# Four stacked attention blocks on one core: bulk loads on a second DMA queue, weights also in idle key and value tiles, softmax denominators normalised per head group

## The chip, the cores and the metric

The kernel runs on one NeuronCore of one Trainium2 chip. The metric is device time in microseconds (us) of one execution, lower is better. Engine names as in the profile: PE is TensorE (matmuls), PEld its weight loads, ACT ScalarE, DVE VectorE, POOL GpSimd, SP SyncE, which here does nothing but issue DMAs.

## The reference

The input `x` has 2048 rows (tokens) of 1024. Two kinds of block alternate, A, B, A, B, each with a layer norm in front and a residual sum behind, and both A blocks share one set of weights, as do both B blocks.

```python
def _A_ref(x, wqkv, w_phi, wo):            # H = 32 heads of Dh = 32
    q, k, v = split(x @ wqkv)
    pq = einsum("bhsd,hdf->bhsf", q, w_phi); pk = einsum("bhsd,hdf->bhsf", k, w_phi)
    phi_q = concat([softmax(pq), softmax(-pq)]); phi_k = concat([softmax(pk), softmax(-pk)])
    kv = einsum("bhsf,bhsd->bhfd", phi_k, v);  z = einsum("bhsf->bhf", phi_k)
    o = einsum("bhqf,bhfd->bhqd", phi_q, kv) / (einsum("bhqf,bhf->bhq", phi_q, z)[..., None] + 1e-6)
    return o @ wo
def _B_ref(x, wqkv, wo):
    q, k, v = split(x @ wqkv)
    p = softmax(einsum("bhqd,bhkd->bhqk", q, k) * Dh ** -0.5)
    return einsum("bhqk,bhkd->bhqd", p, v) @ wo
x = x + _A_ref(_layernorm(x), ...);  x = x + _B_ref(_layernorm(x), ...)     # and both once more
```

A is linear attention: it needs one sum over all tokens (`kv`, `z`) before the first query can be answered. B is ordinary softmax attention over all 2048 keys, 32 heads.

## The kernel before, in words

**How the order comes about.** The kernel is one Python function that plays a clock while it emits instructions (class `Clock`, lines 110 to 190). Each piece of work is a generator that yields operations with an assumed duration and, for DMAs, an assumed latency (`DMA_LAT`, 2.2 us, line 33; 5 or 6 us for the big ones). An operation is written to its engine's stream when the played clock gets there. Every engine, SP's and POOL's streams included, then runs its stream strictly in that order; a wait on the chip that is longer than was assumed holds up everything behind it.

**The layers.** Layers 0 and 2 are A blocks, 1 and 3 are B blocks. Tokens go in four chunks of 512 (`c`), which are 16 tiles of 128 (`t`). For an A block `build_AK` (line 622) computes keys and values of a chunk and adds to `kv`, `build_PQ` (747) the queries, `build_DN` (770) numerator and denominator, `build_AO` (867) the output projection. For a B block `build_BP` (885) makes keys (tiles `K2a`, `K2b`), queries (written to DRAM, `qd`) and values (`Vc`), and `build_BO` (1047) does the output projection. At the very start `build_fold` (564) multiplies `w_phi` into the key and query weights of A; the raw weights lie in the value tiles `Vc` meanwhile, and the products go to DRAM (`wf`).

**Attention of a B block.** It goes in 18 visits (`VISITS`, line 210), each a group of 4 or 2 query tiles against some key chunks for half of the heads: 8 units of two heads each. A unit's step is two exponentials (ACT, line 1187) of 128 x 1024, with the score matmuls ahead (PE, line 1207, into the `ring` banks) and value and row-sum matmuls behind (PE, line 1243, into the one bank `acc`). `finish_unit` (978) then empties `acc` through DVE: line 990 copies, or line 986 (a helper, shown as L351) adds a partial result that `part_load1` fetched from DRAM (`pd`). A unit that isn't its query group's last stores its partial result to `pd`. Visits 9 to 18 are "last": there the row sums of each unit go by DMA to DRAM (`dn`), back to 128 partitions (`rc`, two DMAs, line 1012), through one DVE reciprocal (line 1015), to DRAM again (`rn`, two DMAs, line 1017), back as a broadcast into a buffer `R` (two DMAs, lines 1021 and 1023), and POOL multiplies the result into `oTB` (line 1033). The DMAs wait one for the other on SP. Visits 13 and 14 are the shortest "last" ones: query group 3 against key chunk 3 alone, 2 steps a unit.

**Background.** All other matmuls (projections) are a list of tasks; `pick` (1281) takes the first that has its inputs and its weights. Of the weights, which come as blocks of 1 MB (`slab`), four are held; `slab_plan` (503) loads the one that is needed next into the place of the one that is needed last.

**Queues.** Every DMA is issued by SP (`dma`, line 332), the 1 MB loads among them; the transposes of layer-normed tiles too (336). POOL issues none. POOL does the power for the layer norm's 1/sqrt (412), additions in `build_DN` (846) and the normalisation. Work buffers of 2 KB a partition (`blk`, 23 of them) are shared; tokens limit how many of them one kind of use may hold (`t_acc` 3, `t_part` 4, `t_R` 3, line 307).

## Time and profile before

| | us |
|---|---|
| median of the runs shown (2) | 2794.26 (2788.96 to 2799.56) |
| the profiled execution, time of the run | 2795.94 |
| the profiled execution, span | 2794.2 |
| busy in the span: PE, ACT, DVE, POOL | 2321.4, 2095.9, 977.9, 277.6 |
| DMA: bytes, mean rate | 329.84 MB, 118 GB/s |

The span is one execution, from the first instruction to the last. Engine times are sums over stages that are limited by different things, so the prediction reads them stage by stage: the A block ahead of the first attention (0 to 289), attention of layer 1 (289 to 1506), the A block between (1506 to 1668), attention of layer 3 (1668 to 2781) and the end. Within attention the stages are cut at visits. In a row of such a table a number in brackets behind an engine's busy time counts its instructions; the last three numbers are the granted TensorE clock as a share of full speed, the DMA engines' mean busy share, and GB/s.

### The profile page before, as it was taken

The page shows a single profiled execution, that of the slowest core. Times are in us where ns is not written, and L with a number is a line of the kernel's source. Part 1 is how long each engine was busy: PE and PEld are TensorE (multiplying, and loading weights), DVE is VectorE, ACT ScalarE, POOL GpSimd, SP SyncE. Part 2 cuts the span into 40 slices and gives each one's busy share as a digit, 9 for nine tenths or more (in the row PEclk, how much of TensorE's full clock was granted, in tenths as well). Part 3 has the DMA queues.
Part 4 walks back from the last instruction along what each step waited for, and adds up shares of the span by engine and source line. Part 5 has one row for each costly group of instructions (what it writes and reads, how often), then busy time and mean ns, then how long its engine had stood idle before and what let it go on. Part 6 is the DMA issues. An engine that isn't in the chain of part 4 may idle for free. (4 is left out here: it accounts for less than half of the span.)

```text
span 2794.2 us, 67944 instructions
## 1 busy us (share of the span) xinstructions
PE 2321.4 (83%) x28313; PEld 922.3 (33%) x28313; DVE 977.9 (35%) x1885; ACT 2095.9 (75%) x2413; POOL 277.6 (10%) x327
## 2 busy tenths in 40 slices
PE   6987888988998887677888679889899888877888
PEld 4443332333332222233334333333333322123333
DVE  6866431523332133433333654234233221111011
ACT  4341479789998988477996216778799999957998
POOL 1102000101001111110000010000010011111010
PEclk9999998999998798888999889989999978666787
DMA  7334743553443333533125566347434333332111
GB/s 228 90 106 142 208 161 116 160 173 92 130 127 103 104 97 106 142 96 82 40 48 150 167 177 206 128 138 188 135 100 149 98 100 93 90 92 66 36 29 29
DMA packets 376533, 329.84 MB, mean 118 GB/s; under 512 B 174312, under 2 KB 313440, under 8 KB 370976
## 3 DMA queue, kind: packets, MB, share of 16 engines
q1 hardware_dynamic: 376224, 325.50, 40.7%
q8 instruction: 221, 3.62, 0.6%
q14 instruction: 88, 0.72, 0.1%
HBM read 227.86 MB, written 72.34 MB: 107 GB/s over the span
## 5 line engine op out<-in xcount | busy, mean ns | idle before, releaser
L1187 ACT ACTIVATE E<-ring 128x1024 bf16<-128x1024 f32 x2048 | 1920.7, 1101 | 327.6 <-PE ring L1207 235.2
L1243 PE MATMUL acc<-E,V 128*32 128x512 bf16 (+1 forms) x5120 | 720.3, 385 | 82.8 <-DVE blk L351 68.4
L1243 PE MATMUL acc<-E,ones 128*32 128x512 bf16 (+1 forms) x5120 | 720.1, 385 | 0.0
L1207 PE MATMUL ring<-Q,K2b 32*128 32x512 bf16 (+1 forms) x2560 | 446.3, 376 | 149.8 <-ACT E L1187 143.4
L1207 PE MATMUL ring<-Q,K2a 32*128 32x512 bf16 (+1 forms) x2560 | 464.3, 377 | 39.9 <-DMA Q<-qd 27.2
L1243 PEld LDWEIGHTS <-V 128*32 128x32 bf16 x5120 | 212.8, 102 | 395.9 <-issue 364.8
L351 POOL TENSOR_TENSOR oTB<-blk,blk 64x512 bf16<-64x512 f32 (+1 forms) x156 | 167.0, 1071 | 1131.0 <-DMA blk<-rn 1042.8
L1207 PEld LDWEIGHTS <-K2a 32*128 32x128 bf16 x2560 | 123.7, 93 | 464.0 <-issue 423.7
L1207 PEld LDWEIGHTS <-K2b 32*128 32x128 bf16 x2560 | 148.4, 93 | 268.0 <-issue 259.0
L1015 DVE RECIPROCAL rc<-rc 128x8 f32<-128x8 f32 (+1 forms) x156 | 30.1, 193 | 573.3 <-DMA rc<-dn 573.1
L365 PE MATMUL bg<-xnT,slab 128*32 128x512 bf16 x2604 | 190.8, 414 | 28.0 <-ACT blk L758 9.7
L1243 PEld LDWEIGHTS <-ones 128*32 128x32 bf16 x5120 | 203.5, 102 | 0.1
L990 DVE COPY blk<-acc 128x512 f32<-128x512 f32 (+1 forms) x160 | 93.2, 582 | 268.3 <-PE acc L1243 266.4
L365 PEld LDWEIGHTS <-slab 128*32 128x32 bf16 x4232 | 121.1, 101 | 172.8 <-issue 88.7
L365 PE MATMUL bg<-slab,xnT 128*32 128x512 bf16 x1940 | 146.0, 424 | 30.9 <-DVE kvacc L351 10.6
L351 DVE TENSOR_TENSOR blk<-blk,acc 128x512 f32<-128x512 f32 x128 | 87.5, 683 | 228.8 <-PE acc L1243 158.0
L351 POOL TENSOR_TENSOR blk<-blk 128x256 bf16<-128x256 f32 x96 | 70.0, 733 | 754.3 <-DVE blk L351 404.5
L368 PE MATMUL ring<-slab,xnT 128*128 128x512 bf16 x464 | 114.0, 387 | 9.9 <-DVE kvacc L351 2.6
L351 DVE TENSOR_TENSOR blk<-blk,bg 128x512 bf16<-128x512 bf16 x110 | 75.3, 684 | 129.0 <-PE bg L365 115.7
L365 PE MATMUL bg<-kvacc,slab 128*32 128x512 bf16 x1580 | 109.0, 391 | 12.6 <-DVE K2b L346 9.3
L365 PE MATMUL bg<-slab,oTB 128*32 128x512 bf16 x1500 | 108.7, 413 | 10.0 <-DVE blk L351 8.9
L368 PEld LDWEIGHTS <-xnT 128*128 128x128 bf16 x795 | 77.9, 99 | 114.1 <-issue 17.7
(111 smaller groups left out, 1927.7 us busy)
## 6 DMA issues: line engine op xcount, KB each, us to landing
slab<-in_B_wqkv_dram SPq DMA_DIRECT2D x48, 1024.0 KB
pd<-blk SPq DMA_DIRECT2D x128, 256.0 KB
blk<-pd SPq DMA_DIRECT2D x128, 256.0 KB
slab<-in_A_wo_dram SPq DMA_DIRECT2D x16, 1024.0 KB
Q<-qd SPq DMA_DIRECT2D x256, 64.0 KB
slab<-wf_pq SPq DMA_DIRECT2D x14, 1024.0 KB
Q<-qd SPq DMA_DIRECT2D x112, 128.0 KB
x<-blk SPq DMA_DIRECT2D x48, 256.0 KB
```

Source lines behind the costliest of these rows:

```text
L351: return ("op", e, cost, lambda x: eng(x).tensor_tensor(out=o, in0=a, in1=b, op=op))
L365: nc.tensor.matmul(o[js], lhsT=l[:, js], rhs=r, start=st, stop=sp, tile_position=(0, 32 * j), skip_group_check=True)
L368: nc.tensor.matmul(o, lhsT=l, rhs=r, start=st, stop=sp, skip_group_check=True)
L990: yield ("op", "V", c_ps(n), lambda e: nc.vector.tensor_copy(out=a, in_=acc_t[:, 0:n]))
L1015: yield ("op", "V", 0.2, lambda e: nc.vector.reciprocal(out=rc[:, 0:m], in_=rc[:, 0:m]))
L1187: yield ("op", "S", c_act(2 * n), lambda x: nc.scalar.activation(out=E[:, :, 0:n], in_=ring_t[buf][:, :, 0:n], func=ACT.Exp, scale=INV_SQR ...
L1207: nc.tensor.matmul(ring_t[bufs[e]][:, j, i * n:(i + 1) * n], lhsT=K2[e][c][r, u.g, m, :], rhs=u.Q[r, e, 0:n], start=True, stop=True, tile_ ...
L1243: nc.tensor.matmul(u.acc[r0 + 32 * j:r0 + 32 * j + 32, 0:n], lhsT=lh, rhs=E[:, j, i * n:(i + 1) * n], start=first, stop=final, tile_positi ...
```

## The change

It has three parts, and new numbers for the played clock. (1) `bulk` issues weight loads, the spills of layer-normed activations and their reloads on POOL's DMA queue; all smaller DMAs stay on SP. (2) The value and key tiles are split by halves of the heads, and while they aren't needed for keys and values, each group of them serves as a further place for weights (`Slot`, `slot_open`, `slot_retire`); a task that writes keys or values first retires the place. `slab_plan` may look at 12 blocks ahead in place of 6. (3) `norm` treats the two units of a head group together: their four rows of sums go through one chain, and the broadcast reciprocals land in the unused halves of the two result buffers, so `R` goes. `oTB` tiles become `blk` buffers, of which there are 28; `t_acc` is 5, `t_part` 6. The folded weights' order at the start, the place of `build_PQ(2, 0)` and the assumed durations change as well.

```diff
-DMA_LAT = 2.2
+DMA_LAT = 2.4
+RATE = {"D": 200e3, "P": 150e3}
...
-    return (124 + n) / 960.0
+    return (150 + n) / 960.0
...
-    return 0.2 + 0.0034 * n
+    return 0.18 + 0.0022 * n
...
-    K2 = [[sb(f"K2{x}{c}", [P, G, 2, P]) for c in range(NC)] for x in "ab"]
-    Vc = [sb(f"V{c}", [P, 4, D]) for c in range(NC)]
+    K2 = [[[sb(f"K2{x}{c}{h}", [P, 4, 2, P]) for h in range(2)] for c in range(NC)] for x in "ab"]
+    Vc = [[sb(f"V{c}{h}", [P, 4, C]) for h in range(2)] for c in range(NC)]
...
+    slots = [Slot([sb(f"slab{i}", [P, PO, C])[:]], 8, True) for i in range(4)]
+    vs_no, ks_no = {}, {}
+    for h in range(2):
+        for i in range(2):
+            vs_no[h, i] = len(slots)
+            slots.append(Slot([Vc[2 * i + j][h][:] for j in range(2)], 4, False))
+            ks_no[h, i] = len(slots)
+            slots.append(Slot([K2[x][2 * i + j][h][:].rearrange("p g m n -> p (g m n)").rearrange(
+                "p (a n) -> p a n", n=C) for j in range(2) for x in range(2)], 2, False))
...
-    t_q, t_acc, t_part, t_R, t_tmp = tok(2), tok(3), tok(4), tok(3), tok(3)
+    t_q, t_acc, t_part, t_R, t_tmp, t_ot = tok(2), tok(5), tok(6), tok(2), tok(3), tok(8)
...
-    def dma(o, i, lat=DMA_LAT):
-        return ("op", "D", 0.07, lambda e: nc.sync.dma_start(out=o, in_=i), lat)
+    qbusy = {"D": 0.0, "P": 0.0}
+
+    def queue(q, kb):
+        def lat():
+            qbusy[q] = max(qbusy[q], clk.now) + kb * 1024 / RATE[q]
+            return qbusy[q] - clk.now + DMA_LAT
+        return lat
+
+    def dma(o, i, kb=4):
+        return ("op", "D", 0.07, lambda e: nc.sync.dma_start(out=o, in_=i), queue("D", kb))
+
+    def bulk(o, i, kb):
+        return ("op", "P", 1.0, lambda e: nc.gpsimd.dma_start(out=o, in_=i), queue("P", kb))
...
-        yield dma(slab_t[i][:], src, 6.0)
+        n = len(sl.parts)
+        for j, part in enumerate(sl.parts):
+            ld = bulk(part, src[:, j * sl.per:(j + 1) * sl.per, :], 1024 // n)
+            yield ld if j == n - 1 else ld[:4] + (0.0,)
...
+    def slot_retire(i):
+        sl = slots[i]
+        if not sl.avail:
+            return True
+        if sl.users or sl.loading:
+            return False
+        for x in [x for x in slab_of if slab_of[x] == i]:
+            del slab_of[x]
+            slab_ready.pop(x, None)
+        sl.avail = False
+        return True
...
-            yield dma(dnd[i][:, 0:n], a[d0:d0 + 64:32, :])
-            for j in range(2):
-                yield ("op", "D", 0.07, lambda e, j=j: nc.sync.dma_start(
-                    out=rc[64 * j:64 * j + 64, 0:m], in_=dnd[i][j, 0:n].rearrange("(p e) -> p e", e=m)),
-                    DMA_LAT * j)
-            yield ("op", "V", 0.2, lambda e: nc.vector.reciprocal(out=rc[:, 0:m], in_=rc[:, 0:m]))
-            for j in range(2):
-                yield ("op", "D", 0.07, lambda e, j=j: nc.sync.dma_start(
-                    out=rnd[i][j, 0:n].rearrange("(p e) -> p e", e=m), in_=rc[64 * j:64 * j + 64, 0:m]),
-                    DMA_LAT * j)
-            rc_s.give(rc)
-            yield ("op", "D", 0.07, lambda e: nc.sync.dma_start(
-                out=r[n0:n0 + 32, :], in_=rnd[i][0:1, 0:n].to_broadcast([32, n])), 0.0)
-            yield dma(r[n0 + 32:n0 + 64, :], rnd[i][1:2, 0:n].to_broadcast([32, n]))
...
+    def norm(x0, x1):
+        u, a0, tk0, b0 = x0
+        _, a1, tk1, b1 = x1
...
+        yield ("op", "D", 0.07, lambda e: nc.sync.dma_start(out=dn[0:2, :], in_=a0[64:128:32, :]), 0.0)
+        yield dma(dn[2:4, :], a1[0:64:32, :], 20)
+        yield dma(rc[:, 0:m], dn[:].rearrange("a (p e) -> (a p) e", e=m), 20)
+        yield ("op", "V", 0.2, lambda e: nc.vector.reciprocal(out=rc[:, 0:m], in_=rc[:, 0:m]))
+        yield dma(rn[:].rearrange("a (p e) -> (a p) e", e=m), rc[:, 0:m], 20)
+        rc_s.give(rc)
+        for j in range(4):
+            dst = (a1[32 * j:32 * (j + 1), :] if j < 2 else a0[32 * j:32 * (j + 1), :])
+            yield ("op", "D", 0.07, lambda e, j=j, dst=dst: nc.sync.dma_start(
+                out=dst, in_=rn[j:j + 1, :].to_broadcast([32, n])), queue("D", 256) if j == 3 else 0.0)
+        yield from ot_slot(u)
+        o = ot_ap(u.l, u.q, u.g)
+        yield tt("P", c_pool(n), o[0:64, ot_cols(u)], a0[0:64, :], a1[0:64, :], ALU.mult)
+        yield tt("P", c_pool(n), o[64:128, ot_cols(u)], a1[64:128, :], a0[64:128, :], ALU.mult)
...
-            build_AK(0, 0)
+            build_AK(0, 0, (0, 1), (0,))
             build_fold(("pk", 1))
+            build_AK(0, 0, (0, 1), (1,))
...
-NBLK = 23
+NBLK = 28
```

Three places of the instruction order, before and after. The first is SP in layer 3, among the short visits 13 and 14. Rows are DMAs; `dn`, `rc`, `rn` are the stations of the row sums, `Q<-qd` loads queries, `blk<-pd` a partial result; the shapes are those of the first operand. Before:

```order
L333 DMA dn_373<-blk_93 2x512
L333 DMA blk_92<-pd_2_3_360 128x512
L1017 DMA rn_388<-rc_151 64x8 x2
L1012 DMA rc_148<-dn_373 64x8 x2
L1021 DMA blk_110<-rn_388 32x512
L333 DMA blk_110<-rn_388 32x512
L333 DMA dn_374<-blk_92 2x512
L333 DMA blk_103<-pd_2_4_361 128x512
L1017 DMA rn_381<-rc_148 64x8 x2
```

After:

```order
L1103 DMA dn_1_390<-blk_110 2x512
L367 DMA dn_1_390<-blk_124 2x512
...
L367 DMA blk_128<-pd_2_0_369 128x512
L367 DMA blk_107<-pd_2_1_370 128x512
L367 DMA rc_161<-dn_1_390 128x16
L1011 DMA Q_136<-qd_2_1_274 128x512
L1012 DMA Q_136<-qd_2_1_274 64x512
L367 DMA Q_136<-qd_2_1_274 64x512
L367 DMA rn_1_398<-rc_161 128x16
```

The chain of one unit was seven DMAs, and two units' chains stood interleaved; now eight DMAs serve two units, with other loads between its stations.

The second place is POOL at the start of the program, where the layer norm's power (`st<-st,nhalf`) for the first tiles stands. Before:

```order
L1079 MEMSET E_120 128x1024
L1082 MEMSET VA_134 128x8
...
L412 TENSOR_TENSOR st_138<-st_138,nhalf 128x1
L412 TENSOR_TENSOR st_139<-st_139,nhalf 128x1
L412 TENSOR_TENSOR st_140<-st_140,nhalf 128x1
```

After:

```order
L370 DMA V_90<-in_A_wqkv_dram 128x4x512
L370 DMA slab_133<-in_A_wqkv_dram 128x8x512
L370 DMA V_91<-in_A_wqkv_dram 128x4x512
L370 DMA slab_134<-in_A_wqkv_dram 128x8x512
L370 DMA V_94<-in_A_wqkv_dram 128x4x512
L370 DMA V_95<-in_A_wqkv_dram 128x4x512
L449 TENSOR_TENSOR st_150<-st_150,nhalf 128x1
L370 DMA V_92<-in_A_wqkv_dram 128x4x512
L449 TENSOR_TENSOR st_151<-st_151,nhalf 128x1
```

Six loads, 4 MB together, now stand ahead of the first power, and the second half of the first weights to be folded (`V_92`) behind it.

The third place is POOL near the end of layer 1's attention, where it multiplies (`64x256`) the last query groups. Before, these multiplications follow each other:

```order
L351 TENSOR_TENSOR oTB_131<-blk_103,blk_106 64x256
L351 TENSOR_TENSOR oTB_131<-blk_96,blk_95 64x256
L351 TENSOR_TENSOR oTB_132<-blk_107,blk_109 64x256
L351 TENSOR_TENSOR oTB_132<-blk_90,blk_98 64x256
L351 TENSOR_TENSOR oTB_133<-blk_102,blk_89 64x256
```

After, weights for layer 2 go into value and key tiles between them:

```order
L388 TENSOR_TENSOR blk_102<-blk_112,blk_107 64x256
L370 DMA V_90<-wf_pk_67 128x2048
L370 DMA V_92<-wf_pk_67 128x2048
L370 DMA K2a_74<-in_A_wqkv_dram 128x2x512
L370 DMA K2b_82<-in_A_wqkv_dram 128x2x512
...
L370 DMA K2a_80<-wf_pq_66 128x1024
L370 DMA K2b_88<-wf_pq_66 128x1024
L388 TENSOR_TENSOR blk_102<-blk_116,blk_124 64x256
```

Here twelve loads in a row (the dots leave out six) have come to stand between two multiplications. Over the program SP's stream goes from 127 transfers of 1 MB and 312 + 312 `rc` and `rn` DMAs to none of 1 MB and 78 + 78; POOL's gets 161 DMAs of 105 MB in all. The order of the matmuls, counted at every 32nd of the attention's score matmuls, differs by at most some 30 background matmul groups of about 2,400.

277 lines of the change are left out of this document (150 added, 127 removed).

## Prediction

> **What bounds the kernel now.** I read the page's busy times first, then a table by stages, then the exponentials alone by the same stages, then the waits and the DMA issues of the worst stage.
>
> ```profile
> PE 2321.4 (83%) x28313; PEld 922.3 (33%) x28313; DVE 977.9 (35%) x1885; ACT 2095.9 (75%) x2413; POOL 277.6 (10%) x327
> 0.00:289.00 289.00, 228.19 (x1538) 123.29 (x1538) 204.59 (x389) 99.25 (x178) 30.28 (x50) 0.96 0.49 144
> 808.00:1098.00 290.00, 233.04 (x2744) 75.93 (x2744) 77.60 (x150) 245.69 (x270) 40.15 (x34) 0.85 0.37 105
> 1098.00:1205.00 107.00, 76.38 (x859) 27.93 (x855) 42.43 (x80) 64.59 (x72) 19.13 (x17) 0.87 0.46 120
> 1205.00:1506.00 301.00, 234.21 (x4444) 113.80 (x4443) 93.94 (x176) 254.80 (x291) 31.96 (x39) 0.89 0.28 67
> 1506.00:1668.00 162.00, 119.38 (x762) 59.96 (x750) 100.81 (x199) 30.97 (x56) 18.48 (x27) 0.89 0.63 185
> 2185.00:2435.00 250.00, 218.33 (x2316) 63.13 (x2305) 47.34 (x99) 236.89 (x257) 36.81 (x30) 0.82 0.34 95
> 2435.00:2534.00 99.00, 71.09 (x586) 19.86 (x586) 19.23 (x39) 61.07 (x65) 17.49 (x14) 0.65 0.34 90
> 2534.00:2604.00 70.00, 57.45 (x1028) 26.57 (x1029) 10.21 (x25) 59.53 (x65) 9.94 (x10) 0.77 0.22 56
> ```
>
> Behind the stage's length stand PE, PEld, DVE, ACT, POOL, the granted clock, the DMA share and GB/s. The A blocks (0 to 289, 1506 to 1668) are PE's: 228 and 119 us busy. In attention ACT sets the pace where nothing else is late. Where it runs unhindered shows in the exponentials alone:
>
> ```profile
> 1098.00:1205.00 107.00, 61.75 (x64) 0.87 0.46 120
> 2435.00:2534.00 99.00, 61.07 (x65) 0.65 0.34 90
> 2604.00:2781.00 177.00, 176.58 (x192) 0.74 0.18 29
> ```
>
> 192 in 177 us are 0.92 us each, so 64 need 59 us. The short visits 13 and 14 hold 64 in each layer and took 107 and 99 us. Neither PE (76 and 71 busy) nor ACT fills them. Who does, in layer 3, show the waits and the issues of that stage:
>
> ```profile
> DVE rc L1015 <- DMA rc<-dn: 33.6, 15, 4.8
> DVE blk L351 <- DMA blk<-pd: 25.1, 7, 7.5
> PE acc L1243 <- DVE blk L351: 19.6, 9, 5.2
> POOL oTB L351 <- DMA blk<-rn: 57.5, 11, 10.4
> ```
>
> ```profile
> blk<-rn SPq DMA_DIRECT2D x28, 64.0 KB
> rn<-rc SPq DMA_DIRECT2D x30, 2.0 KB
> rc<-dn SPq DMA_DIRECT2D x28, 2.0 KB
> dn<-blk SPq DMA_DIRECT2D x15, 4.0 KB
> ```
>
> ```profile
> L1012 SPq DMA_DIRECT2D rc<-dn x28: 461/587/772, 2439.9 to 2529.0; - x28
> L333 SPq DMA_DIRECT2D dn<-blk x15: 487/498/503, 2437.8 to 2529.7; - x15
> L1017 SPq DMA_DIRECT2D rn<-rc x312: 445/541/1922, 824.5 to 2774.8; - x156
> L1021 SPq DMA_DIRECT2D blk<-rn x156: 306/333/807, 827.4 to 2776.1; - x156
> ```
>
> The three numbers behind the colon are minimum, median and maximum in ns of one issue, the upper two rows' in this stage, the lower two's in the whole run. SP spends 28 x 0.587 + 15 x 0.498 + 30 x 0.541 + 28 x 0.333 = 49 us of 99 on issuing chains, and between the stations it waits, with the loads of partial results (`blk<-pd`) and queries behind it in the same stream. DVE, held 33.6 us for `rc`, and those late partial results keep `acc` full, PE can't add the next sums, and ACT runs dry. So here SP's stream is the bound, not an engine's arithmetic.
>
> **Part 3, the merged chain.** A unit's seven issues become eight for two, so four. `dn` and the broadcasts stay one and two a unit; one `rc` and one `rn` are left where four were for two units, so each unit saves 1.5 of each: for some 14 units 21 x 0.587 + 21 x 0.541 = 24 us of SP. Of 49 us, 25 are left, and half of the stops. Partial results have six tokens instead of four. With 59 us of exponentials in 99, SP should no longer decide, though the first unit of a pair now waits for the second and keeps its buffer. I take 66 us for the stage in layer 3 and 74 in layer 1, where ACT has 64.59 - 61.75 = 3 us of other work and background runs beside it, against floors of 59 and 62: (99 - 66) + (107 - 74) = **66 us**. Bounds: 85 at the floors, below zero if pairing holds buffers longer than it saves (a rival). The visit behind it (2534 to 2604) starts with that backlog, 70 us for 59.5 of ACT: **8 us**, at most 11.
>
> Of the other "last" visits ACT's idle time is what can go. 1205 to 1506: 301 - 254.8 = 46; 808 to 1098: 290 - 245.7 = 44; 2185 to 2435: 250 - 236.9 = 13. Here chains are spread over longer units (four steps and more), so only part of the waiting is theirs; the rest is background that PE does while ACT waits, and the order of matmuls hardly changes. I take half: **23 + 22 + 6 us**, between zero and 103.
>
> **Parts 1 and 2, loads.** 127 transfers of 1 MB leave SP's stream. Their issues are short (0.39 us), but what stands behind them in the same queue may land later for them:
>
> ```profile
> L333 SPq DMA_DIRECT2D slab<-in_B_wqkv_dram x48: 367/392/612, 220.7 to 2201.7; - x48
> PE ring L1207 <- DMA Q<-qd: 15.7, 7, 6.4
> PE ring L1207 <- DMA Q<-qd: 13.7, 6, 6.3
> PE bg L368 <- DMA xnT<-blk: 9.6, 1, 9.6
> PE ring L568 <- DMA V<-in_A_wqkv_dram: 8.4, 1, 8.4
> PE bg L568 <- DMA V<-in_A_wqkv_dram: 5.9, 1, 5.9
> ```
>
> The first two waits are of 289 to 631 and 1668 to 2006, where attention begins and the first queries come late; the third is at the layer boundary (1506 to 1668), the last two in the first 19 us. Weights themselves don't appear as a PE wait, since a task is only emitted once its weights are assumed present; that 22 fewer MB come in therefore counts nothing by itself. Queries behind smaller traffic: half of 29.4 and some of the 6.3 that the boundary has, **16 us** (0 to 29). Boundary: PE idles 162 - 119.4 = 43; I take the transposes' wait, **10 us** (0 to 43). Start: PE waits 14.3 us for weights. Now the x tiles head SP's queue, and PE begins with values; their weights are second on POOL, and POOL's power for the first tile stands behind 4 MB of issues. **3 us**, from 14 gained to 10 lost.
>
> The gains add up to 66 + 8 + 23 + 22 + 6 + 16 + 10 + 3 = 154 us.
>
> **What is added.** 161 bulk issues on POOL, an operation that this trace has not. Nearest rows: an SP issue of such a load, 0.39 us, and POOL's own multiplication,
>
> ```profile
> L351 POOL TENSOR_TENSOR oTB<-blk,blk 64x512 bf16<-64x512 f32 (+1 forms) x156 | 167.0, 1071 | 1131.0 <-DMA blk<-rn 1042.8
> ```
>
> 1.07 us. From above it is bounded by POOL being held until the data have come: 1 MB at the 144 GB/s of the first stage is 7 us. I take 1.07, as it is POOL's own: 172 us, and POOL goes from 278 to 450 busy of some 2,650, still mostly idle. That is hidden unless something stands behind a run of loads: powers, additions and multiplications. A run of twelve then costs 13 us of POOL. Behind it wait first the layer norm's second half on DVE and the transposes, so the next chunk's matmuls; or a multiplication, so an output projection, which mostly has other background before it. Eleven runs of 4 MB or more stand in POOL's stream; at some 2 us each of them reaching PE I charge 20 us (0 to 195, the rival below). The extra DVE reciprocals are fewer, 78 for 156, with twice the elements, at 0.2 us each; the halved weight tiles cost no matmul. The copies into them are as before.
>
> **Sum.** 2794.2 - 154 + 20 = 2660 us of span. The execution's own time is 2795.94, 1.7 above its span, and the median 2794.26; between them the difference is below anything argued here, so I predict **2660 us**, 4.8% less.
>
> **Rivals.** (a) *More goes than I took*: with SP unblocked the granted clock rises as well, 0.65 in the worst stage and 0.82 to 0.89 in other "last" ones. All lost times above (85 + 11 + 46 + 44 + 13 + 43 + 29 + 14) are 285 us; 70% of them would be 200, so 2594. For it: the unhindered stretch keeps ACT at 177 of 177 with a clock of 0.74. Against: much of it is PE's background in front of ACT.
>
> (b) *A second queue moves nothing forward*: bulk and small transfers still meet in the DMA engines, 63% busy at the boundary. The 16, 10 and 3 us vanish, and half of the 45 in layer 1's "last" visits, where loads also run: 154 - 29 - 22 = 103 is left, and 2794 - 103 + 20 = 2711. For it: the shares above; against: engines aren't full, and a wait of 6.4 us for 128 KB looks like standing in line. The Trainium skill (DMA: Bandwidth & Descriptors, "Issuing engines are not separate DMA queues") states just this: DMAs of all issuers run interleaved on the same 16 engines, and a further issuer saves only issue time. By that rule the time would be this rival's.
>
> (c) *Pairing only moves the wait*: the first unit's buffer waits for its partner, `acc` stays full as before, and the 74 us of the short visits and the one behind stay: 2734. Against: 28 `blk` buffers instead of 23, no `R`, tokens 5 and 6 instead of 3 and 4.
>
> (d) *Slower: POOL becomes what SP was.* If a bulk load holds POOL until its data have landed, the runs of 4 MB and more, 56 MB together, hold it 56 / 0.144 = 389 us. If half of that reaches PE through late layer norms and multiplications, the charge is 195 instead of 20: 2794 - 154 + 195 = 2835. It decides from 154 us on, that is 1 us of lost time per bulk DMA. For it: in the order six loads stand ahead of the first power, and twelve between two multiplications. Against: a load is emitted when its place is assumed free, and PE has other tasks. The Trainium skill (SBUF — State Buffer, "SBUF: two separate sides") names a mechanism by which it would happen: descriptors of a POOL-issued DMA are written by POOL's cores, which are locked out while DVE runs certain two-port operations. DVE is busy 205 of the first 289 us and 101 of 162 at the boundary; how many of its operations are such ones no row here shows.
>
> **How the numbers follow.** Forecast (2610 to 2700) 0.45; (a) 0.12; (b) 0.18; (c) 0.10; (d) 0.15. The forecast's own range is 2610 to 2700. Leaving out half of (a)'s lower end and most of (d) gives 2580 to 2780 for 8 in 10. Faster by over 2%, about what a measurement of this kernel can tell from no change, means below 2738: forecast, (a), most of (b) and half of (c), 0.77. Within 2% (to 2850): the rest of both and half of (d), 0.15. Slower: 0.08, where (d) takes more than half of the held time.
>
> **What would show it.** Right: 64 exponentials in 62 to 75 us in both pairs of short visits, DVE's wait for `rc` at half its present total or less (34 us in the stage above), no PE wait over 4 us for queries. Wrong: `POOL <- DMA` or layer norm rows with idle times of 10 us behind bulk DMAs and PE waiting for `xnT`; PE waiting for `acc` as long as now; bulk DMA instructions of several us on POOL; or the first PE matmul later than 30 us.

## The result, and the profile after

The changed kernel takes **2665.1 us** in the median (2664.74 to 2665.47) where the kernel before took 2794.26: a ratio of 0.954 (95% interval 0.946 to 0.962). The profiled execution's span is 2663.0 us. The page of after, its busy times and its DMA queues (packets, MB, the packets' time as a share of 16 engines' span):

```profile
PE 2292.7 (86%) x28268; PEld 913.2 (34%) x28268; DVE 961.8 (36%) x1787; ACT 2085.9 (78%) x2415; POOL 411.2 (15%) x510
...
q1 hardware_dynamic: 253424, 192.29, 26.7%
q0 software_dynamic: 26384, 110.11, 13.1%
```

PE and ACT have nearly the work they had (29 and 10 us less of 2321 and 2096), so most of the 131 us that the span lost are idle time of theirs. POOL's queue (q0) now carries 110 MB. The stages of after, cut at the same visits as the prediction's table:

```profile
0.00:308.00 308.00, 233.95 (x1544) 123.88 (x1545) 201.38 (x383) 97.50 (x178) 75.46 (x118) 0.92 0.56 160
824.00:1068.00 244.00, 218.82 (x2712) 72.33 (x2715) 75.31 (x131) 240.26 (x266) 43.91 (x40) 0.92 0.42 124
1068.00:1161.00 93.00, 73.90 (x875) 27.19 (x871) 44.00 (x74) 64.25 (x75) 29.27 (x25) 0.87 0.56 153
1161.00:1437.00 276.00, 227.24 (x4536) 112.10 (x4532) 100.24 (x173) 250.81 (x285) 40.94 (x57) 0.93 0.29 74
1437.00:1579.00 142.00, 116.10 (x756) 59.25 (x749) 88.40 (x177) 34.19 (x65) 35.99 (x52) 0.90 0.48 127
2101.00:2338.00 237.00, 214.91 (x2246) 60.68 (x2248) 42.93 (x79) 236.27 (x258) 38.16 (x31) 0.81 0.33 98
2338.00:2412.00 74.00, 63.23 (x623) 18.32 (x627) 17.73 (x31) 59.76 (x66) 20.25 (x16) 0.73 0.42 121
2412.00:2471.00 59.00, 52.56 (x1034) 24.52 (x1027) 9.99 (x21) 59.00 (x66) 9.39 (x10) 0.90 0.22 64
```

In visits 9 to 12 of both layers (rows 2 and 6) and visit 15 of layer 3 (the last row) ACT is now busy for all but 4 us at most; in visits 15 to 18 of layer 1 (row 4) it idles for 25 us where it did for 46. The short visits of layer 3 fell from 99 to 74 us, those of layer 1 (row 3) only from 107 to 93, with 29 us of ACT idle left. The A block at the start (row 1) grew from 289 to 308 us for nearly the same PE work, 228 and 234 us. So two things moved: the "last" visits gained, and something in the first stage was lost.

SP in the short visits of layer 3, by line (minimum, median, maximum ns of one issue), and two waits of that stage (us in all, times, longest):

```profile
L367 SPq DMA_DIRECT2D rn<-rc x8: 320/342/1186, 2337.4 to 2402.4; - x8
L367 SPq DMA_DIRECT2D dn<-blk x8: 483/496/500, 2341.2 to 2408.9; - x8
...
L367 SPq DMA_DIRECT2D rc<-dn x8: 344/518/576, 2345.5 to 2411.7; - x8
```

```profile
L1111 SPq DMA_DIRECT2D blk<-rn x32: 318/417/437, 2341.8 to 2406.9; - x32
```

```profile
POOL blk L388 <- DMA blk<-rn: 66.3, 8, 20.6
...
DVE rc L1106 <- DMA rc<-dn: 10.3, 3, 5.7
```

The other eight `dn` issues stand on line 1103. At 0.5 us for the 16, the chains take 8 x 0.518 + 8 x 0.342 + 16 x 0.5 + 32 x 0.417 = 28 us of SP, where they took 49, and DVE's wait for `rc` is 10.3 us where it was 33.6. POOL still waits 66 us for reciprocals, and in that stage the trace puts no engine's wait down to POOL.

The loss at the start is one place above all. SP's stream and PE there, and the stretch in windows of 10 us:

```profile
167.56 15.82 SPq L373 DMA_TRANSPOSE xnT<-blk  x2
```

```profile
183.49 1.03 PE L405 MATMUL ring<-slab,xnT 128*128 128x512 bf16 x2 [13.10 <-DMA xnT<-blk]
```

```profile
150.00:160.00 10.00, 9.69 (x72) 5.43 (x71) 9.29 (x18) 3.93 (x8) 7.10 (x10) 1.00 1.00 322
160.00:170.00 10.00, 8.07 (x64) 4.70 (x64) 8.17 (x14) 5.19 (x11) 5.50 (x8) 1.00 0.96 157
170.00:180.00 10.00, 0.39 (x7) 0.21 (x4) 1.99 (x3) 0.82 (x2) 0.00 (x0) 0.71 0.96 220
180.00:190.00 10.00, 5.32 (x19) 2.05 (x20) 1.05 (x3) 1.67 (x3) 0.56 (x1) 0.61 0.92 163
```

When the folds end, key and value tiles open as places for weights, and POOL issues a run of bulk loads between 147 and 165 us. From 150 us on the DMA engines are full (share 0.92 to 1.00), two transposes that SP starts at 167.56 hold it for 15.8 us, and PE stops for 13.1 us for want of `xnT`.

### The profile page after: what moved, and what is told of

The parts are those of the page before. It is cut to its first block, busy times and chain, and to the rows that moved or that the text cites. A ratio compares the mean times of both kernels' runs of the same rounds, so it can differ in the third digit from the quotient of the medians.

```text
span 2663.0 us, 67052 instructions
## 1 busy us (share of the span) xinstructions
PE 2292.7 (86%) x28268; PEld 913.2 (34%) x28268; DVE 961.8 (36%) x1787; ACT 2085.9 (78%) x2415; POOL 411.2 (15%) x510
## 3 DMA queue, kind: packets, MB, share of 16 engines
q1 hardware_dynamic: 253424, 192.29, 26.7%
q0 software_dynamic: 26384, 110.11, 13.1%
## 4 chain that ended last, share of the span: by engine, by line
PE 49%; ACT 17%; issue 7%; DMA 4%; DVE 4%; SPq 1%; POOL 0%; ACTq 0%; POOLq 0%; DVEq 0%
PE bg L402 16%; ACT E L1257 15%; PE acc L1313 13%; PE ring L1277 12%; PE ring L405 4%; PE bg L405 3%; DVE blk L388 1%; DMA rc<-dn 1%; DMA xnT<-blk 1%; DMA dn<-blk 1%; ACT blk L705 1%; ACT blk L809 1%; DVE K2b L383 1%; DMA blk<-pd 0%; PE ring L867 0%
## 5 line engine op out<-in xcount | busy, mean ns | idle before, releaser
L1313 PE MATMUL acc<-E,V 128*32 128x512 bf16 (+1 forms) x5120 | 707.8, 377 | 10.9 <-DVE blk L388 8.6
L1313 PE MATMUL acc<-E,ones 128*32 128x512 bf16 (+1 forms) x5120 | 707.8, 378 | 0.0
L388 POOL TENSOR_TENSOR blk<-blk,blk 64x512 bf16<-64x512 f32 (+1 forms) x156 | 166.1, 1065 | 773.9 <-DMA blk<-rn 717.8
L402 PE MATMUL bg<-slab,blk 128*32 128x512 bf16 x2596 | 174.3, 386 | 6.8 <-DVE blk L388 5.1
L402 PE MATMUL bg<-slab,xnT 128*32 128x512 bf16 x1740 | 124.3, 407 | 14.2 <-ACT blk L705 7.8
L405 PE MATMUL ring<-slab,xnT 128*128 128x512 bf16 x416 | 103.6, 391 | 22.4 <-DMA xnT<-blk 13.1
L402 PEld LDWEIGHTS <-blk 128*32 128x32 bf16 x2968 | 82.6, 98 | 80.9 <-issue 22.8
L710 DVE TENSOR_REDUCE sm<-blk 128x32 f32<-128x1024 bf16 x64 | 77.5, 1211 | 90.7 <-ACT blk L705 86.7
L402 PE MATMUL bg<-xnT,slab 128*32 128x512 bf16 x1424 | 101.0, 397 | 10.4 <-DVE K2b L383 5.8
L405 PE MATMUL bg<-slab,xnT 128*128 128x512 bf16 x301 | 78.9, 409 | 30.0 <-DMA xnT<-blk 22.4
```

The costliest lines, as they stand in the source:

```text
L388: return ("op", e, cost, lambda x: eng(x).tensor_tensor(out=o, in0=a, in1=b, op=op))
L402: nc.tensor.matmul(o[js], lhsT=l[:, js], rhs=r, start=st, stop=sp, tile_position=(0, 32 * j), skip_group_check=True)
L405: nc.tensor.matmul(o, lhsT=l, rhs=r, start=st, stop=sp, skip_group_check=True)
L710: yield ("op", "V", c_sb(1024), lambda x: nc.vector.reduce_sum(out=sm[:, 0:32], in_=e3, axis=AX.X))
L1313: nc.tensor.matmul(u.acc[r0 + 32 * j:r0 + 32 * j + 32, 0:n], lhsT=lh, rhs=E[:, j, i * n:(i + 1) * n], start=first, stop=final, tile_positi ...
```

## The experiments

**Theory.** The "last" visits gain because the merged chain frees SP's stream (C). The bulk loads on a queue of their own meet the transposes and small DMAs in the same DMA engines, in bursts, and cost what the start lost (F, called B in e4's expectation; it took its full shape after the first four runs). Rivals: the second queue is what pays (Q); POOL's in-order stream is what costs (D). Ratios are against the kernel before, on the same chip, with 95% intervals; the first row rests on two runs of each kernel, the others on four and more, so its interval is the widest.

| run | what it is | ratio |
|---|---|---|
| changed kernel | | 0.9538 [0.946, 0.962] |
| e1_chain_alone | before + merged chain | 0.9646 [0.963, 0.967] |
| e2_unit_chain | changed, chain per unit again | 0.9898 [0.987, 0.993] |
| e3_bulk_on_sp | changed, bulk DMAs on SP | 0.9351 [0.933, 0.937] |
| e4_no_extra_places | changed, four weight places | 0.9419 [0.940, 0.944] |
| e5_pool_stand_in | e3, POOL held by dummies | 0.9363 [0.934, 0.939] |
| e6_one_at_a_time | changed, one planned load at a time | 0.9491 [0.947, 0.951] |
| e7_sp_no_extra | e3 and e4 together | 0.9414 [0.939, 0.943] |
| e8_clock_alone | before + new durations | 0.9986 [0.997, 1.000] |
| e9_old_tokens | e7, old limits of buffers | 0.9682 [0.967, 0.970] |
| e10_pool_rows | changed, loads cut in eight | 0.9374 [0.936, 0.939] |
| e11_sp_raw_first | e3, first weights ahead of x | 0.9307 [0.930, 0.932] |
| e12_pool_paced | changed, POOL pauses after loads | 0.9419 [0.940, 0.944] |

And the lengths of stages in us, cut at the exponentials of each profiled run:

| stage | before | after | e1 | e2 | e3 | e4 | e7 | e9 |
|---|---|---|---|---|---|---|---|---|
| first A block | 289 | 308 | 288 | 313 | 292 | 296 | 296 | 297 |
| layer 1, visits 1-8 | 519 | 516 | 522 | 515 | 510 | 522 | 518 | 516 |
| 9-12 | 289 | 245 | 253 | 282 | 243 | 244 | 244 | 260 |
| 13-14 | 107 | 93 | 99 | 92 | 89 | 92 | 90 | 101 |
| 15-18 | 301 | 276 | 281 | 303 | 260 | 262 | 260 | 282 |
| A block between | 162 | 142 | 159 | 151 | 135 | 155 | 154 | 130 |
| layer 3, visits 1-8 | 516 | 522 | 516 | 523 | 519 | 503 | 500 | 522 |
| 9-12 | 250 | 237 | 237 | 249 | 238 | 235 | 236 | 242 |
| 13-14 | 99 | 74 | 88 | 81 | 72 | 75 | 73 | 92 |
| 15-18 | 248 | 238 | 244 | 249 | 237 | 237 | 236 | 255 |

**e1: the chain alone.** The kernel before with `norm`; the buffers of `R` become result buffers.

```diff
-    t_q, t_acc, t_part, t_R, t_tmp = tok(2), tok(3), tok(4), tok(3), tok(3)
+    t_q, t_acc, t_part, t_R, t_tmp = tok(2), tok(5), tok(4), tok(2), tok(3)
...
+        if not u.fast:
+            grp.setdefault(kq, []).append((u, a, token, b))
+            if len(grp[kq]) == 2:
+                clk.start(norm(*grp.pop(kq)))
+            return
```

> The kernel before with the merged chain alone: one chain for the two units of a head group, no R buffers (their place goes to result buffers, five tokens instead of three); bulk loads stay on SP, four weight places, old durations of the played clock. Theory C (the freed SP stream of the 'last' visits is what pays, and the chain frees it): of the 132 us that visits 9 to 18 of both layers gave, some 100 appear, so about 2694 us; visits 13 and 14 take 75 to 95 us in each layer; the first 289 us and the boundary stay as before. Rival Q (the second queue pays, by taking 1 MB loads out from under the small ones): at most 50 us less than before, about 2745. Rival S (longer chains only pay with the buffers and tokens that the whole change brings): 2780 or more.

2700.7 us, ratio 0.9646: 99 us of the 129 for the chain with its two more result buffers (0.0354 x 2794). The first A block and the boundary stay at 288 and 159, as expected; the short visits of layer 1, at 99, are longer than the 75 to 95 expected. Over the run DVE's wait for `rc` falls from 573.1 to 190.0 us, PE's for queries (29.4 before) hardly:

```profile
DVE rc L1048 <- DMA rc<-dn: 190.0, 57, 7.0
...
PE ring L1226 <- DMA Q<-qd: 28.9, 12, 6.8
```

**e2: everything but the chain.** `finish_unit` as before, with `R`.

```diff
-        if not u.fast:
-            grp.setdefault(kg, []).append((u, a, token, b))
...
+            for j in range(2):
+                yield ("op", "D", 0.07, lambda e, j=j: nc.sync.dma_start(
+                    out=rc[64 * j:64 * j + 64, 0:m], in_=dn[j, :].rearrange("(p e) -> p e", e=m)),
+                    DMA_LAT * j)
```

> The changed kernel with a chain for each unit again (seven small DMAs a unit, a buffer for the reciprocals, three tokens for them); bulk loads stay on POOL and weights still go into idle key and value tiles. Theory C: the 132 us of the 'last' visits are mostly lost again, so 2755 to 2775 us, with DVE waiting 25 us or more for rc in visits 13 and 14 of layer 3. Rival Q: with no 1 MB load on SP the chains run fast enough as they are, at most 40 us are lost, 2705 or less.

2770.6 us, ratio 0.9898. In the short visits of layer 3 DVE's wait for `rc` is back, and longer than the 33.6 us before, yet the stage takes 81 us and not 99. What went is ACT's wait for `acc`; first before, then e2's two waits:

```profile
ACT E L1187 <- PE acc L1243: 29.7, 7, 15.8
```

```profile
DVE rc L1070 <- DMA rc<-dn: 40.7, 13, 5.9
...
ACT E L1275 <- PE acc L1331: 11.8, 7, 5.7
```

So for the total C holds from both sides: without the chain 0.990, with it 0.954. Taking 1 MB loads out of SP's stream does not make the old chains fast enough; Q falls. By stages it holds for the longer "last" visits, which go back to 282 and 303 us in layer 1 and 249 and 249 in layer 3. In the short visits 15 us in layer 1 (after: 14) and 18 in layer 3 (after: 25) come without the merged chain. This run has the five result buffers and six partial results too, so there the buffers are the likelier cause; e9 takes them away.

**e3: bulk DMAs on SP.** All else, the played order too, stays.

```diff
-        return ("op", "P", 1.0, lambda e: nc.gpsimd.dma_start(out=o, in_=i), queue("P", kb))
+        return ("op", "P", 1.0, lambda e: nc.sync.dma_start(out=o, in_=i), queue("P", kb))
```

> The changed kernel with every bulk DMA issued by SP instead of POOL, at the same place of the played clock, so that the order of all else stays. Theory C: issuing costs SP some 0.4 us a load in place of 0.6 to 0.9 on POOL; the same bytes meet in the same 16 DMA engines; so within 20 us of the changed kernel, 2645 to 2685, and the late first matmul (22 us) and the 18 us lost ahead of the first attention stay or shrink. Rival Q: small DMAs stand behind the loads in the queue, 40 us or more are lost, 2705 or more, and PE again waits over 4 us for queries. Rival D (POOL's order holds the layer norm at the start): the start alone gains 10 us and more, the rest is unchanged, about 2650.

2616.9 us, ratio 0.9351, below what any of the three expected: the second queue costs 1.9%, 52 us (48 by the two medians). The same stretch as above, in e3, with the same loads now in SP's order:

```profile
150.00:160.00 10.00, 9.05 (x82) 5.67 (x80) 8.68 (x17) 4.58 (x9) 3.27 (x3) 1.00 0.82 237
160.00:170.00 10.00, 8.03 (x56) 4.26 (x55) 8.78 (x14) 5.24 (x10) 0.00 (x0) 1.00 0.89 274
170.00:180.00 10.00, 8.81 (x62) 4.70 (x61) 7.06 (x13) 3.84 (x7) 0.00 (x0) 1.00 1.06 315
180.00:190.00 10.00, 9.66 (x58) 4.82 (x57) 8.93 (x12) 3.99 (x8) 0.00 (x0) 1.00 0.83 266
```

The DMA engines are about as full (0.82 to 1.06), but they move 273 GB/s on average where they moved 216, and PE is 8 to 9.7 us of 10 busy. The longest issue of these transposes is 3.3 us in e3 and 12.6 in after. I read this as a transpose that now waits only for what was issued ahead of it. The stage is 292 us instead of 308, and visits 15 to 18 of layer 1 gain 16 us.

**e4: no extra places.** `slot_open` no longer sets `avail`.

```diff
     def slot_open(i):
-        slots[i].avail = True
         slab_plan()
```

> The changed kernel with only the four weight tiles as places for weights, as before: the idle key and value tiles never open for them. Theory B (the bursts of loads that opening them sets off collide with transposes, at 147 to 165 us and at the end of layer 1's attention): the stage ahead of the first attention takes 290 to 298 us instead of 308, and the whole 2645 to 2660. Rival P (the weights held there feed the background and shorten the boundary and visits 9 to 18 of layer 1): the boundary goes back from 142 to about 160 us and layer 1's last visits lose some 30, so 2700 or more.

2637.2 us, ratio 0.9419. The first stage is 296 us, as theory B said, and the total lower than it gave; the boundary goes back to 155, but the visits behind it take 503 instead of 522, so what the boundary gains with extra places (14 us) the first eight visits give back.

**e5: is it POOL's stream?** e3, but POOL touches each tile where it issued the DMA and fills a scratch tile.

```diff
+            if store:
+                nc.gpsimd.tensor_copy(out=stand[:, 0:32].rearrange("p (a b) -> p a b", b=4), in_=i[:, :, ::P])
+            else:
+                nc.gpsimd.memset(o[:, :, ::P], 0.0)
+            nc.gpsimd.memset(stand[:], 0.0)
+            nc.sync.dma_start(out=o, in_=i)
```

> The run with all bulk DMAs on SP (2617 us), but at each place where the changed kernel's POOL issues one, POOL now touches the same tile (32 elements a partition, so that it waits for what the DMA there waited for; a load's place is overwritten afterwards by the load) and then fills a scratch tile, together some 0.6 to 1 us, so that POOL's stream is held about as in the changed kernel while the bytes go by SP's queue. Theory F (the 48 us between POOL's queue and SP's come from two queues meeting in the DMA engines, where SP's order would have spaced the loads): stays within 15 us of SP's, 2605 to 2632. Rival D (POOL's order does it: powers and multiplications stand behind loads that wait): most of the 48 us come back, 2645 to 2670.

2610.7 us, ratio 0.9363 against e3's 0.9351: the same. The stand-ins hold POOL for less than the issues did (74 us against 121), but they wait as long for their tiles (879 us in all against 900), and POOL's multiplications wait for reciprocals as before. In e5 and in after:

```profile
L377 POOL MEMSET stand<- 128x160 f32 x161 | 43.8, 272 | 0.7
...
L376 POOL MEMSET slab<- 128x32 bf16 x57 | 13.7, 240 | 531.0 <-PE bg L411 318.9 <-PE bg L414 97.6 <-PE ring L414 95.8
```

```profile
L370 POOL DMA_DIRECT2D slab<-in_B_wqkv_dram x28 | 25.7, 919 | 249.8 <-PE ring L1277 167.6 <-PE ring L405 26.0 <-PE bg L402 23.1
L370 POOL DMA_DIRECT2D V<-in_B_wqkv_dram x16 | 12.1, 759 | 6.6 <-PE bg L402 4.4 <-PE ring L405 1.0 <-PE ring L1277 1.0
```

D falls: what stands behind a bulk issue in POOL's stream costs nothing here. What costs is by which queue the bytes go.

**e6: one load at a time.** `slab_plan` starts no load while one is under way on the played clock, and is called again at each load's end.

```diff
+        slab_plan()
...
-            if best is None:
+            if best is None or any(x.loading for x in slots):
```

> The changed kernel, bulk loads on POOL's queue and extra places as they are, but the planner starts a weight load only when no other is under way (on its played clock), so runs of ten loads become a load every 9 us or so. Theory F (bursts of POOL's queue against transposes and small DMAs): the wait of 13 us at 183 us goes, the stage ahead of the first attention takes 288 to 296 us, and the whole 2620 to 2645. Rival D: POOL's issues are as many as before and spaced, so a gain of 15 us at most, 2650 to 2665. Rival W (weights now come late, PE's background dries up): slower than the changed kernel, 2680 or more.

2647.1 us, ratio 0.9491: better than the changed kernel's median, but its interval lies within the changed kernel's, and less than F expected. The wait of 13 us is gone, yet the first stage took 316 us, since more of the A block's matmuls moved in front of the first attention (246 us of PE instead of 234); visits 1 to 8 took 502 instead of 516. As a test of F it is weak.

**e7: both undone.**

> The changed kernel with all bulk DMAs on SP and only the four weight tiles as places for weights. Alone these two gave 48 and 28 us off the changed kernel's time. If they are two separate costs, 2585 to 2595. Theory F (both are the same collisions in POOL's queue, so one cure is enough, and on SP the extra places then pay a little at the boundary): 2610 to 2640, with the boundary at about 155 us instead of 135.

2625.4 us, ratio 0.9414. The edits are those of e3 and e4. Their gains don't add: on SP the extra places help (0.9351 with, 0.9414 without), on POOL's queue they cost (0.9538 with, 0.9419 without). So the harm needs both: with four places POOL's queue costs nothing (0.9419 on it, 0.9414 on SP). A run of loads that opened places set off is what the first stage shows. It is not all: visits 15 to 18 of layer 1 lose 16 us as well, and where PE stops there (1218 to 1232 us, see the end of this document) POOL had issued two 1 MB loads since 1200.

**e8: the new durations alone.**

```diff
-DMA_LAT = 2.2
+DMA_LAT = 2.4
...
-    return (124 + n) / 960.0
+    return (150 + n) / 960.0
...
-    return 0.2 + 0.0034 * n
+    return 0.18 + 0.0022 * n
```

> The kernel before with nothing but the new assumed durations of DMA, copies out of PSUM and POOL. The theories of the chain and of the queue agree that this is worth little, 2780 to 2805 us; a rival (the played order was wrong by its old durations, and the new numbers alone carry the rest that the chain does not) gives 2755 or less.

2781.4 us, ratio 0.9986: nothing, as expected.

**e9: the old limits.** Between e1 (0.9646) and e7 (0.9414) lay 65 us with no name. e7 with:

```diff
-    t_q, t_acc, t_part, t_R, t_tmp, t_ot = tok(2), tok(5), tok(6), tok(2), tok(3), tok(8)
+    t_q, t_acc, t_part, t_R, t_tmp, t_ot = tok(2), tok(3), tok(4), tok(2), tok(3), tok(8)
```

> The run with bulk DMAs on SP and four weight places (0.9414 of before), with the old limits of three result buffers and four fetched partial results (t_acc 3, t_part 4) in place of five and six. The chain alone gave 0.9646; what lies between is the shared pool of buffers, these limits, the split tiles, the queues in the played clock and the order of the start. Theory T (the limits let the two units of a group wait for each other without filling acc): most of the 65 us come back, 0.955 to 0.965, 2670 to 2695 us, with the short visits at 95 us or more in layer 1 and 85 or more in layer 3. Rival K (the played clock's queues, which space loads and fetch queries earlier, do it): 0.941 to 0.947, 2630 to 2645.

2709.3 us, ratio 0.9682: 75 us come back, even a little more than theory T gave. `acc`, in e7 and then in e9 (busy, mean ns, idle before and what ended it), and ACT in the short visits of layer 3 of e9:

```profile
L1312 PE MATMUL acc<-E,V 128*32 128x512 bf16 (+1 forms) x5120 | 707.3, 378 | 10.5 <-DVE blk L388 8.2
```

```profile
L1312 PE MATMUL acc<-E,V 128*32 128x512 bf16 (+1 forms) x5120 | 713.4, 382 | 25.7 <-DVE blk L388 23.1
```

```profile
DVE rc L1105 <- DMA rc<-dn: 34.1, 6, 8.0
ACT E L1256 <- PE acc L1312: 32.4, 7, 8.5
```

With three result buffers, two units that wait for one chain leave one for the next: `rc` is late again and ACT waits 32.4 us there for `acc`, where it waited 11.8 in e2, though DVE waited more for `rc` there. So the merged chain needs its buffers, and the short visits need them more than the chain: 101 and 92 us with the chain and the old limits, 92 and 81 with the new limits and no merged chain (e2). Queue and places, in which the two differ as well, move these stages little: 93 and 74 in after, 90 and 73 in e7. Two things stay open: e1 had five result buffers already, so a part of these 75 us lies in its 99; and the 65 us between e1 and e7 may be the sixth and fifth partial result, the larger pool or the queues in the played clock, which no run splits.

**e10: loads in eight pieces.** One DMA of 128 KB for each block of rows.

```diff
-        return ("op", "P", 1.0, lambda e: nc.gpsimd.dma_start(out=o, in_=i), queue("P", kb))
+        return ("op", "P", 1.0 if kb > 128 else 0.5, lambda e: nc.gpsimd.dma_start(out=o, in_=i), queue("P", kb))
...
-        for j, part in enumerate(sl.parts):
-            ld = bulk(part, src[:, j * sl.per:(j + 1) * sl.per, :], 1024 // n)
-            yield ld if j == n - 1 else ld[:4] + (0.0,)
+        for j in range(8):
+            ld = bulk(sl(j), src[:, j, :], 128)
+            yield ld if j == 7 else ld[:4] + (0.0,)
```

> The changed kernel with each weight load on POOL's queue cut into eight DMAs of 128 KB, one for each of the eight row blocks (1 KB in a row), where it had one to four. In the changed kernel's records POOL's queue moved its bytes in packets of 4.2 KB on average (110.11 MB in 26384), SP's in the run with all on SP added 85520 packets for the same bytes, 1.3 KB each; while ten loads were under way the two transposes beside them advanced by 434 and 314 packets of 256 B in 5 us each, against 1024 that each tile needs. Theory P (an engine takes packets of the two queues in turn, so a transpose of many small packets pays a large packet's time for each of its own; smaller packets let it through): if the packets become 1 KB, the wait at 183 us falls below 6 us and the total to 2620 to 2645, in spite of some 700 more issues on POOL. Rival F2 (whatever is in the second queue takes its share of bytes, packet size does not matter) with POOL held longer by the issues: 2665 to 2700. Rival D2 (some 700 issues of 0.5 us or more now hold POOL's powers and multiplications, 350 us in all): 2720 or more.

2625.2 us, ratio 0.9374: where theory P put it, but not by its reason. The loads' packets stayed at 4 KB (23040 of them, against 20736), so their size was not tested. What changed is POOL's time for a load, eight issues in place of one to four, on the chip and, at 4 us, in the played clock:

```profile
L370 POOL DMA_DIRECT2D slab<-in_B_wqkv_dram x224 | 120.0, 544 | 209.2 <-PE bg L402 113.5 <-PE bg L405 76.8 <-PE ring L405 8.3
```

8 x 0.544 = 4.4 us for 1 MB, so a run of loads comes at 240 GB/s at most, not at one load in 0.9 us (my estimate from that row). POOL was 665 us busy, and that did no harm: rival D2 falls too.

**e12: pacing alone.** The loads in one to four DMAs as in the changed kernel, a pause of POOL behind each; the played clock counts 4 us for a load.

```diff
+                nc.gpsimd.dma_start(out=o, in_=s_)
+                for _ in range({1: 12, 2: 5, 4: 1}[n]):
+                    nc.gpsimd.memset(stand[:], 0.0)
```

> The changed kernel with its weight loads on POOL's queue as they were (one to four DMAs each), but after each DMA POOL fills a scratch tile for a while, so that a weight load of 1 MB holds POOL some 4 us in all, as long as its eight issues did in the run with loads cut into rows, and the played clock counts 4 us for it as there. In that run the packets did not become smaller (23040 of 4 KB, against 20736), so its gain of 1.6% over the changed kernel cannot be their size. Theory R (POOL's longer issue paced the loads to 1 MB in 4 us or more and so broke up the bursts): 0.935 to 0.942, 2615 to 2640 us, the transposes' longest issue below 7 us. Rival X (cutting a load into eight pieces is what helps, by the way it is spread over the engines): no better than the changed kernel, 0.948 to 0.956, 2650 to 2675. Rival D (a POOL held this long puts off powers and multiplications): above 2675.

2638.7 us, ratio 0.9419, at the edge of theory R's range and below rival X's; rival D falls once more. The transposes' issues (minimum, median, maximum ns), in after and in e12:

```profile
L373 SPq DMA_TRANSPOSE xnT<-blk x48: 1232/1263/12607, 11.9 to 1843.8; - x48
```

```profile
L375 SPq DMA_TRANSPOSE xnT<-blk x48: 1232/1257/3481, 15.3 to 1822.5; - x48
```

The longest falls from 12.6 to 3.5 us, the stage is 297 us instead of 308, and 1.2 of the 1.9% come back. That is what breaking up the bursts should do; but the played clock counts the pauses too, so the order of instructions may have moved with them, and no run splits the two.

**e11: a better version.** e3 with the first weights to be folded ahead of the x tiles in SP's stream.

```diff
-        yield bulk(raw[k].parts[0], src[:, 0:4, :], 512)
+        yield bulk(raw[k].parts[0], src[:, 0:4, :], 512)[:4] + (0.0,)
...
-    clk.start(phi_load())
-    clk.start(first_x())
...
+    clk.start(load_raw(("pk", 0)))
+    clk.start(phi_load(), 0.0001)
+    clk.start(first_x(), 0.0002)
```

> All bulk DMAs on SP, extra places open (0.9351 of before), and the first half of the first weights that are folded at the head of SP's stream, ahead of the x tiles, so that PE folds while the first layer norm and transposes run. PE's first matmul was at 22.9 us there; the folding of one weight block is some 10 us of PE work that now fits in front. If the start is PE's from the first matmul on: the stage ahead of the first attention 282 to 288 us instead of 292.5, the ratio 0.931 to 0.934, 2602 to 2610. Rival: the first x tile lands later behind 512 KB and what PE folds early it lacks later, no gain, 0.934 to 0.938.

2605.1 us, ratio **0.9307**, the fastest of all: 7% below before, 2.4% below the changed kernel. The first stage takes 285 us. PE at the start:

```profile
4.30 0.61 PE L634 MATMUL bg<-ident,V 128*128 128x128 bf16 x4 [4.30 <-DMA V<-in_A_wqkv_dram]
...
25.62 0.27 PE L647 MATMUL bg<-E,K2a 128*128 128x128 bf16 x1 [11.66 <-DMA E<-in_A_w_phi_dram]
```

PE begins at 4.3 us instead of 22.9, and then waits 11.7 us for the small `w_phi` DMAs, whose last stand late in SP's stream: a next thing to move, not tried here.

## Why the prediction was right, and where it was not

The sum came out within 5 us (2660 for 2665.1). Point by point, in us:

| term | predicted | measured |
|---|---|---|
| short visits 13 and 14 | 33 + 33 | 25 (layer 3) + 14 (layer 1) |
| visit 15 of layer 3 | 8 | 11 |
| visits 15-18, layer 1 | 23 | 25 |
| visits 9-12, layer 1 and 3 | 22 + 6 | 45 + 13 |
| queries, visits 1-8 of both layers | 16 (a part at the boundary) | 3 and -6 |
| boundary | 10 | 20 |
| start | 3 | -18 |
| bulk issues on POOL | -20 | see below |

**Part 3** was the right place and size: its terms were 125 us together, visits 9 to 18 gave 132. Within them two sizes were off, and by luck they cancel: the short visits gave 39 of 66, visits 9 to 12 gave 58 of 28. I took half of ACT's idle time in visits 9 to 12; nearly all went, since it was the chain's. And the 74 us taken for layer 1's short visits left out that the next A block's exponentials stand in ACT's stream there, behind background matmuls:

```profile
ACT blk L705 <- PE bg L405: 18.7, 2, 15.0
```

That is read from after's waits (1068 to 1161), not tested by a run. The larger error is of attribution: the prediction gave the merged chain the whole gain and the tokens half a sentence. The chain with the buffers that `R` left is worth 99 us; under the old limits the chain and the other changes around it give 89 together (e9, 0.9682), and the limits then bring 75. For the short visits, the largest term of the sum, two steps did not hold, "here SP's stream is the bound" and the one from DVE's wait for `rc` to a full `acc`: in e2, with a chain for each unit on SP and 40.7 us of waiting for `rc`, the stage took 81 us. The rival "pairing only moves the wait" was wrong for this kernel, but at three result buffers it is partly what e9 shows.

**Part 1** had its sign wrong. I expected 16 + 10 + 3 - 20 = 9 us from the loads' move; the comparison of e3 with the changed kernel shows a loss of 52. The step that failed is "what stands behind them in the same queue may land later for them": with the loads in SP's queue (e3) PE waits for no query and, behind its start, at most 2.1 us for `xnT`, and on a queue of their own the loads ran beside the transposes. The charge of 20 us priced POOL's stream (issues of 0.54 to 0.93 us, within the bounds and below the 1.07 taken), which e5 shows to cost nothing; what two queues do to each other in full DMA engines (150 to 190 us) was the cost to price. The start's bounds (14 gained to 10 lost) did not hold 18 lost; in e3 the stage is 292 us, so 3 us of the loss are not the queue's and the rest are.

The waits for queries are gone, as the prediction asked, but they are gone in e3 too, with the loads on SP; so it was not the loads' new queue that removed them. Neither the chain alone (28.9 us left in e1) nor the new durations alone (26.7 in e8) did it; what did stays open. Nor did the stages of the first eight visits get much shorter:

```profile
289.00:808.00 519.00, 463.80 (x5798) 172.28 (x5796) 178.73 (x334) 432.75 (x487) 27.65 (x41) 0.96 0.49 147
```

```profile
308.00:824.00 516.00, 465.66 (x5768) 173.10 (x5768) 177.75 (x333) 434.05 (x489) 51.59 (x71) 0.95 0.45 129
```

PE has 464 and 466 us of work in 519 and 516, the longest of all engines: a wait taken from it came back elsewhere. The step "queries, half of 29.4" took a wait of an engine for time of the stage.

**Part 2** was argued to count nothing by its bytes. With the loads on SP it is worth 0.6%, on POOL's queue it costs 1.2%: what it does depends on the queue. Its boundary gain is given back by the visits behind it (142 + 522 in after, 155 + 503 in e4).

**Rivals.** (b) had the right object: DMAs of both queues meet in the same engines. The Trainium skill (DMA: Bandwidth & Descriptors, "Issuing engines are not separate DMA queues") says that a further issuer saves only issue time; the runs go beyond it, since the second queue cost 52 us here. With four places for weights it cost nothing (e7). (d) did not come: no bulk issue held POOL longer than 1.1 us, and e5 shows the holding to be harmless. Of the signs named, `rc` waits, 64 exponentials in 74 us (layer 3) and the first matmul at 22.4 us (it was at 5.9 before) came out on the right side, 93 us in layer 1 and PE waiting 13 us for `xnT` on the wrong one. So the main term was right in place, in size by two errors that cancel, and the total by luck besides: with the loads on SP (e3) the change would have given 181 us instead of the 134 forecast, and the queue, which no term held, took 52 of them.

## What to carry to other kernels

A small chain of dependent DMAs in an in-order stream is priced by its stations and by the buffers held meanwhile: merging two chains paid in full only with more buffers to wait in, and where units are short the buffers seem to have done most of it. A long wait in a trace is not a price: DVE waited longer for `rc` in e2 than before, in a stage 18 us shorter. A second DMA queue is no second path: before bulk loads get their own, look at what runs in the same microseconds, at transposes above all. The DMA engines' share alone does not tell, since it was as high with all on SP; in one queue the order of the stream protected the urgent small transfer here, in two pacing the loads helped. To tell whether the issuing engine or its transfers cost, issue them elsewhere and let the engine do stand-ins.

## What the runs showed of the hardware

- The same weight loads went in packets of 4096 B on POOL's queue (20736, 207 ns each on average) and nearly all of 1024 B on SP's (77824 more in e3, 53 ns each): the same time for a byte. Cutting a load into eight DMAs left POOL's packets at 4096 B.
- Beside them, transposes can crawl. Counted from the packet records of after, 5 us each:

```
us        POOL's queue: packets, mean ns    SP's queue: packets, mean ns
155-160   394, 133                          1056, 26
165-170   123, 719                          434, 45
170-175   214, 240                          314, 45
180-185   23, 116                           1921, 55
1215-1220  87, 282                          739, 105
1220-1225  30, 2747                         236, 151
1230-1235  15, 109                          1653, 23
```

  A tile's transpose has 1024 packets of 256 B. At 165 to 175 us both queues advance, SP's by 75 packets a us, where nearly alone it does 384 (180 to 185, 1715 of them of 256 B); at 155 a tile went through beside 394 packets in 5 us. The Trainium skill (DMA: Bandwidth & Descriptors, "Queues, rings and completion order") states that each DMA engine takes whole packets from its queues in turn. The counts agree that both go on together, not that they alternate one by one; whether a packet of the records is one of that page no run shows, and none here changed the packets' size. Why it was slow at 165 and not at 155 stays open.
- At 1220 to 1225 us 30 packets of mostly 8 KB took 2.7 us each, where 8 KB take 0.41 on average; there DVE waited 13.8 us for `rc` and PE 11.8 for DVE. Why both slowed so much stays open too.
- POOL's issues of bulk DMAs, of 1 MB and of 256 KB (minimum, median, maximum ns), are short and steady; they do not wait for the data, which land 7.3 us later for 1 MB. They go by the number of pieces more than by bytes, as the third row shows, 1 MB in 128 rows of 8 KB where the first has 1024 of 1 KB:

```profile
L370 POOL DMA_DIRECT2D slab<-in_B_wqkv_dram x28: 882/896/1101, 198.3 to 2104.3; - x28
...
L370 POOL DMA_DIRECT2D K2a<-in_B_wqkv_dram x12: 704/704/709, 73.8 to 1687.7; - x12
...
L370 POOL DMA_DIRECT2D slab<-wf_pk x5: 587/592/603, 893.6 to 1213.1; - x5
```
